# New figures in a kernel's list scheduler: traced durations, one DMA queue, hops between engines, GpSimd and two-operand VectorE work apart

## The chip, the cores and the metric

The kernel runs on one core of a Trainium2 chip. The metric is the device time of one execution in microseconds. The kernel before takes 753.49 us (median of 3 runs, 753.48 to 754.42).

## What is computed

Three layers follow each other, on 2 batches of 768 tokens, all in float32.

1. Clustered attention: 8 heads of 64. Each query and key is given to the nearest of 16 centroids (arg max of the cosine), and a query sees only the keys of its own cluster: `scores = where(q_assign == k_assign, q k^T / 8, -1e9)`, soft max, times v.
2. A mixture of 8 experts with one expert for a token: `e = argmax(x w_gate + modality_bias[modality_id])`, `out = gate * (relu(x w1[e]) w2[e])`, with w1 of 512 x 1024 and w2 of 1024 x 512.
3. A feed-forward layer of 2048: `h = x w_in`, `g = max(h, 0) + alpha * min(h, 0)`, `out = g w_out`. Its weights come as 64-bit floats and are turned into 32-bit ones on the chip.

## The kernel before

**Tiles and loops.** The attention goes by groups of two heads (4 groups in a batch), and in each by 12 units of 128 queries against 768 keys: the scores (`smm`, L946, in `pss`), the negated row maximum on VectorE (L953), the exponential on ScalarE (L965), a split of the result into two 16-bit parts (a high copy, then a low part on GpSimd, L393 on tile p, or on VectorE, L995), a DMA transpose of both parts issued by SyncE (L999, `pt<-p`), and the product with v on TensorE (`avm`, L1007 and L1009). A third of the first batch's units is transposed on TensorE instead. `group_prep` readies the next group meanwhile: transposes, norms (L756 is in that chain), nearest centroids (L840 to L847), the split of v (L913), and moves of 64 partitions to the other 64 (`move`), each on SyncE's DMA queue, GpSimd or ScalarE. After the last group of a batch `route` and `inverse` work out on VectorE, in a long chain of small operations, which token goes to which slot of which expert (the logits are added on L1070).

The experts work in slots of 128 tokens: SyncE loads the expert's weights in 8 parts (conditionally, where the expert is that of the slot before), GpSimd gathers the token rows (L1337), TensorE transposes them (L1345) and multiplies (L1401, L1431). The first 3 slots multiply in full float32; later ones (10) split the weights into a high part on ScalarE and a low part on VectorE (`whl`). GpSimd then gathers the rows back (L1447), TensorE transposes them (L1457), and the feed-forward runs by 16 slices of 128 of the inner 2048 for each batch: first product (L1517), leaky ReLU on VectorE (L1525, L1528), split (`ghl`, ScalarE and GpSimd), second product (L1545). Its weights are put together from 64-bit words on VectorE (L1487 to L1492) and split (`wf`).

**What sets the order.** Nothing of the order is written by hand. Each operation is declared with `S.op`: the engines that can do it with a cost each, what it reads and writes, a priority, and for a DMA its transfer time. `Sched.run` (L182) then plans the whole program on the host, and `emit` issues the operations in the order of their planned starts. Each engine executes its own queue strictly in that order, and waits with semaphores; so a wrong planned time costs nothing by itself, but an operation planned too early stands in the way of the ones behind it. In each step `run` works out for every ready operation the earliest start on its best engine (start + cost + a bias), takes for each engine, of those that start within a window of the earliest (0.03 us, on VectorE 0.3), the one with the lowest priority number, and plans of these the one that starts first. The plan is made in two parts: one up to a branch (L1657) at about 472 us, one for the last stage behind it.

The figures of the planner before: 0.2 us from an engine to any other (`LAT`), 0.127 between dependent VectorE operations, DMAs with an issue of 0.47 or 0.65, 0.65 more, their transfer (all transfers one after another, `dma_free`) and 0.9 to land. The dictionary `N` (L350) holds some fifty settings: ring sizes, offsets of priorities, biases.

Of the kernel before, what the change touches and what calls it, by code (L numbers as in the profile page):

```python
# [13 lines left out]
I32 = mybir.dt.int32  # L14
# [60 lines left out]
class Op:  # L75
    __slots__ = ("idx", "eng", "fn", "prio", "deps", "succ", "ndep", "ready", "start", "end", "bufs", "on", "dma", "bias", "adds", "slack")


class Sched:


    LAT = 0.2
    WIN = 3.41333
    SAME = 0.08
    DSAME = 0.127

    def __init__(self):
        self.ops = []
        self.prio = 0.0
        self.rings = []  # L90
        self.stream = None
        self.bias = {}
        self.win = {}
        self.back = 0.5
        self.warm = [False]
        self.pe_busy = {}
# [10 lines left out]
    def op(self, eng, fn, r=(), w=(), prio=None, dma=None, deps=(), bias=None, slack=0.0):  # L107
# [4 lines left out]
        o.prio = self.prio if prio is None else prio  # L112
# [6 lines left out]
        o.slack = slack  # L119
# [62 lines left out]
    def run(self, t0=0.0):  # L182
        ops = self.ops
        for o in ops:
            o.ndep = 0
            o.ready = t0
# [13 lines left out]
        dma_free = t0  # L200
        hw_free = t0
# [3 lines left out]
        while n_done < total:  # L205
            best = None
            per = {}
            for o in ready:
                at = o.ready
# [47 lines left out]
            end = self.pe_end(st, cost) if e == "PE" else st + cost  # L257
            free[e] = end
            if o.dma is not None and e in o.dma[2:] + (e,) * (len(o.dma) == 2):
                xfer, hw = o.dma[:2]  # L260
                if hw and e != "POOL":
                    hw_free = max(st, hw_free) + (0.47 if hw == "load" else 0.65)
                    xs = hw_free + 0.65
                    free[e] = hw_free + 0.03
                else:
                    xs = end + 0.65
                dma_free = max(xs, dma_free) + xfer
                if hw == "transpose":
                    free[e] = dma_free - 0.93
                end = dma_free + 0.9 + o.slack  # L270
            o.end = end
            ready.remove(o)
            n_done += 1
            for rg, i in o.adds:
                rg.free.append((end + self.LAT, i))
            for b in o.bufs:
                b.left -= 1
                if b.left == 0 and b.ring is not None:
                    b.ring.free.append((max(y.end for y in b.ops) + self.LAT, b.slot))
# [20 lines left out]
def kernel(  # L300
# [49 lines left out]
    N = dict(s1q=2, s1k=2, s2q=2, s2k=2, p=3, p16=5, pt=4, v16=2, wf_early=2, xs=2, whl=3, whl2=3, whi='A', wlo='D', lead=1, tw=1, wdma=1.25, pss=2, ps1=4, sq=1, bd=1.5, bp=0, ulead=4, pa=2, pb=0, nat=3, hi='*', lo='DP', lo0='PPT', vraw=1, mvp=1, mvb=0, epi=1, rM=2, lob=0.5, idle=40, pace=57, mve='PA', wd=0.3, wa=0.03, wp=0.03, wpl=0.03, cs=1, back=2, nld=8, dsame=0.127, lump='cs', mp=90, mps=8, mpn=0, trp=0.5, evp=3, xTs2=0, xtp=9, fl=6, rsh=1, rp0=0, go=-4, so=0, pre=0, fws=5, gs=4, gsl=1, xsl=0, eb=0.8)  # L350
# [4 lines left out]
    S.DSAME = N["dsame"]  # L355
# [22 lines left out]
    def chain(name, r, w, *steps, prio=None):  # L378

        if name in N["lump"]:  # L380
# [3 lines left out]
            S.op({"DVE": sum(0.127 + n / 960.0 for _, n in steps)}, all_, r=r, w=w, prio=prio)  # L384
            return
        for fn, n in steps:
            S.op({"DVE": 0.06 + n / 960.0}, fn, r=r, w=w, prio=prio)
# [10 lines left out]
    def open_pool(name, side="left", space=None, deps=()):  # L398
# [14 lines left out]
        o = S.op({"MEM": 0.0}, fn, deps=deps, prio=-1e9)  # L413
# [9 lines left out]
    def close_pool(name):  # L423
# [4 lines left out]
        return S.op({"MEM": 0.0}, lambda _: pools.pop(name).release(), deps=deps, prio=-1e9)  # L428
# [128 lines left out]
    def consts():  # L557
# [3 lines left out]
            name=nc.get_next_instruction_name(), act_func_set_id=6)), prio=-1e6)  # L561
        S.op({"POOL": 0.9}, lambda e: make_identity(nc, ident.t), w=[ident])
        S.op({"POOL": 0.1}, lambda e: nc.gpsimd.memset(half.t, 0.5), w=[half])
        S.op({"POOL": 0.1}, lambda e: nc.gpsimd.memset(cexp.t, CEXP), w=[cexp])
        S.op({"POOL": 0.1}, lambda e: nc.gpsimd.memset(tiny.t, 1e-30), w=[tiny])
        S.op({"POOL": 0.1}, lambda e: nc.gpsimd.memset(ones_r.t, 1.0), w=[ones_r])
        S.op({"DVE": 0.1}, lambda e: nc.vector.memset(one16.t, 1.0), w=[one16])

        S.op({"POOL": 0.2}, lambda e: iota(iw.t, [[-1, NCL]], NCL), w=[iw])
# [6 lines left out]
        S.op({"DVE": 0.3}, scales, w=[msc])  # L576
# [5 lines left out]
        for i in range(N["v16"]):  # L582
            S.op({"DVE": 0.1}, lambda e, i=i: nc.vector.memset(r_v16.tiles[i][:, :, :, 2 * D:], 1.0),
                 w=[(s2z, ("v", i))], deps=[r_v16.opened], prio=0)
# [3 lines left out]
    def zero(rg, i, view, n, key):  # L588
        S.op({"POOL": 0.1 + n / 1000.0, "DVE": c_dve(n)}, lambda e: ENG[e].memset(view(rg.tiles[i]), 0.0),
             w=[(s2z, key)], deps=[rg.opened])  # L590

    def late_consts():
        S.prio = 2
        S.op({"DVE": 0.2}, lambda e: nc.vector.memset(ones_b.t, 1.0), w=[ones_b])
        S.op({"POOL": 0.3}, lambda e: nc.gpsimd.affine_select(
            out=tri_b.t, in_=ones_b.t, pattern=[[1, P]], compare_op=ALU.is_gt, fill=0.0, base=0,
            channel_multiplier=-1), r=[ones_b], w=[tri_b])
        S.op({"POOL": 0.2}, lambda e: iota(iw8.t, [[-1, E]], E), w=[iw8])
        S.op({"POOL": 0.2}, lambda e: iota(tri8r.t, [[1, E], [-1, E]]), w=[tri8r])
# [1125 lines left out]
```

## Time and profile before

| | |
|---|---|
| median of the runs | 753.49 us |
| profiled execution | 755.47 us |
| its span, first to last instruction | 753.7 us |
| granted TensorE clock, mean | 0.97 |
| busy: TensorE, weight loads | 685.7, 578.5 us |
| busy: VectorE, ScalarE, GpSimd | 541.8, 397.2, 322.9 us |
| DMA | 101.39 MB, 135 GB/s |

The shares over the whole span hide that the stages have different limits; the table by stretches among the rows below has one line for each stage, with the busy time of every engine and the share of the DMA engines (1.0 is all 16 busy). Matmuls overlap, so a busy TensorE may still be below its best. A line such as L393 or L365 is that of a helper (a subtraction, a copy); there the names of the tiles tell the operations apart.

### The profile page before, as it was taken

The page shows a single profiled execution, that of the slowest core. Times are in us where ns is not written, and L with a number is a line of the kernel's source. Part 1 is how long each engine was busy: PE and PEld are TensorE (multiplying, and loading weights), DVE is VectorE, ACT ScalarE, POOL GpSimd, SP SyncE. Part 2 cuts the span into 40 slices and gives each one's busy share as a digit, 9 for nine tenths or more (in the row PEclk, how much of TensorE's full clock was granted, in tenths as well). Part 3 has the DMA queues.
Part 4 walks back from the last instruction along what each step waited for, and adds up shares of the span by engine and source line. Part 5 has one row for each costly group of instructions (what it writes and reads, how often), then busy time and mean ns, then how long its engine had stood idle before and what let it go on. Part 6 is the DMA issues. An engine that isn't in the chain of part 4 may idle for free. (4 is left out here: it accounts for less than half of the span.)

```text
span 753.7 us, 13656 instructions
## 1 busy us (share of the span) xinstructions
PE 685.7 (91%) x5041; PEld 578.5 (77%) x5041; DVE 541.8 (72%) x920; ACT 397.2 (53%) x609; POOL 322.9 (43%) x282
## 2 busy tenths in 40 slices
PE   8778889876888899989889999799999999999997
PEld 8768778765767657447668787699999889999996
DVE  7899889998978865399999896388988632322331
ACT  6778888854758667158769896122322231111112
POOL 5537776553648634001425400554556642222221
PEclk9999999996799999999999999899999999999999
DMA  7779998896999999940814913243343030000002
GB/s 182 174 145 208 168 170 184 150 229 107 220 217 230 189 173 195 294 160 29 292 57 140 330 61 128 77 132 115 115 142 135 14 108 19 1 0 1 1 1 85
DMA packets 167211, 101.39 MB, mean 135 GB/s; under 512 B 133120, under 2 KB 147840, under 8 KB 167136
## 3 DMA queue, kind: packets, MB, share of 16 engines
q1 hardware_dynamic: 164832, 93.04, 51.1%
q0 software_dynamic: 2304, 7.39, 3.6%
q8 instruction: 42, 0.69, 0.4%
q14 instruction: 33, 0.27, 0.1%
HBM read 87.37 MB, written 12.85 MB: 133 GB/s over the span
## 5 line engine op out<-in xcount | busy, mean ns | idle before, releaser
L1545 PE MATMUL ps<-wf,ghl 128*128 128x512 f32 x576 | 138.2, 392 | 1.6 <-POOL ghl L393 1.6
L1545 PEld LDWEIGHTS ps<-wf,ghl 128*128 128x128 f32 x576 | 107.1, 188 | 23.6 <-POOL ghl L393 3.0
L365 ACT ACTIVATE ghl<-g 128x384 fp32r<-128x384 f32 x64 | 33.7, 526 | 158.1 <-DVE g L1528 156.7
L393 POOL TENSOR_TENSOR ghl<-g,ghl 128x384 fp32r<-128x384 f32 x57 | 66.0, 1163 | 118.1 <-ACT ghl L365 118.1
L1525 DVE TENSOR_SCALAR m<-ps,alp 128x384 f32<-128x384 f32 x64 | 39.4, 615 | 106.4 <-PE ps L1517 106.4
L393 POOL TENSOR_TENSOR p<-p,p 128x768 f16<-128x768 f32 x57 | 97.0, 1711 | 37.1 <-ACT p L365 32.5
L965 ACT ACTIVATE p<-pss,nm 128x768 f32<-128x768 f32 x96 | 86.0, 898 | 34.3 <-DVE nm L953 16.3
L393 DVE TENSOR_TENSOR whl<-wst,whl 128x1024 fp32r<-128x1024 f32 x80 | 100.9, 1299 | 3.7 <-ACT whl L365 3.3
L953 DVE TENSOR_REDUCE nm<-pss 128x1 f32<-128x768 f32 x96 | 90.8, 950 | 15.8 <-PE pss L946 9.4
L365 ACT ACTIVATE whl<-wst 128x1024 fp32r<-128x1024 f32 x80 | 83.9, 1060 | 15.5 <-PE ps L1431 7.8
L1007 PEld LDWEIGHTS <-pt 128*128 128x128 f16 x1152 | 61.3, 100 | 34.5 <-DMA pt<-p 28.9
L1007 PE MATMUL ps<-v,pt 128*128 128x65 f16 x1152 | 69.9, 197 | 17.1 <-DMA pt<-p 16.1
L1517 PE MATMUL ps<-x2a,wf 128*128 128x384 f32 x384 | 72.1, 345 | 3.9 <-ACTq L1657 3.9
L946 PE MATMUL pss<-s1k,s1q 128*128 128x384 f32 x192 | 61.0, 400 | 14.4 <-ACT p L965 14.2
L1517 PEld LDWEIGHTS ps<-x2a,wf 128*128 128x128 f32 x384 | 69.9, 194 | 5.4 <-ACTq L1657 4.3
L1517 PE MATMUL ps<-x2b,wf 128*128 128x384 f32 x384 | 69.9, 338 | 0.0
L1517 PEld LDWEIGHTS ps<-x2b,wf 128*128 128x128 f32 x384 | 67.6, 188 | 1.1
L1401 PE MATMUL ps<-whl,xTs 128*128 128x512 f32 x240 | 64.0, 405 | 4.6 <-DVE whl L393 4.5
L1431 PE MATMUL ps<-whl,hTs 128*128 128x512 f32 x240 | 63.0, 399 | 3.1 <-DVE hTs L393 3.1
L1401 PEld LDWEIGHTS ps<-whl,xTs 128*128 128x128 f32 x240 | 45.1, 193 | 15.5 <-DVE whl L393 6.2
L393 POOL TENSOR_TENSOR wf<-tw,wf 128x1024 fp32r<-128x1024 f32 x16 | 40.1, 2507 | 35.5 <-ACT wf L365 35.3
L1431 PEld LDWEIGHTS ps<-whl,hTs 128*128 128x128 f32 x240 | 43.9, 188 | 14.7 <-DVE hTs L393 6.2
(244 smaller groups left out, 1214.4 us busy)
## 6 DMA issues: line engine op xcount, KB each, us to landing
wst<-in_moe_w_dram SPq DMA_DIRECT2D x104, 512.0 KB
wst<-in_moe_w_in_dram SPq DMA_DIRECT2D x8, 1024.0 KB
wst<-in_moe_w_out_dram SPq DMA_DIRECT2D x8, 1024.0 KB
ys_d<-ys SPq DMA_DIRECT2D x13, 256.0 KB
raw<-in_k_dram SPq DMA_DIRECT2D x8, 384.0 KB
raw<-in_q_dram SPq DMA_DIRECT2D x8, 384.0 KB
vraw<-in_v_dram SPq DMA_DIRECT2D x8, 384.0 KB
x_d<-xg SPq DMA_DIRECT2D x8, 384.0 KB
```

The lines of the kernel that those rows point to most:

```text
L365: nc.scalar.activation(out=out, in_=in_, func=AF.Copy)
L393: ENG[e].tensor_tensor(out=out, in0=a, in1=b, op=ALU.subtract)
L946: nc.tensor.matmul(s.t[:, jj, 0:HS], hd["12"[i], "q"].t[:, h, j, qs], hd["12"[i], "k"].t[:, h, jj], start=(i == 0), stop=(i == 1))
L953: S.op({"DVE": c_dve(SEQ)}, lambda e: nc.vector.tensor_reduce(out=nm.t, in_=s.t[:, :, 0:HS], axis=AX.XY, op=ALU.max, negate=True), r=[s], ...
L965: S.op({"ACT": c_act(SEQ) + 0.04}, lambda e: nc.scalar.activation(out=p.t, in_=s.t[:, :, 0:HS], func=AF.Exp, bias=nm.t), r=[s, nm], w=[p])
L1007: nc.tensor.matmul(o[:, c], pv, vv[:, D:VW], start=(i == 0), stop=(i == 2 * C - 1))
L1401: nc.tensor.matmul(hps[jj].t, lhs(xT, a, ci), rhs(ch, w_, cols), start=(ci == 0 and i == 0), stop=(ci == 3 and i == len(parts) - 1))
L1431: nc.tensor.matmul(yp.t, lhs(hT, a, f), rhs(4 + f // 2, w_, slice((f % 2) * 512, (f % 2 + 1) * 512)), start=(f == 0 and i == 0), stop=(f = ...
L1517: nc.tensor.matmul(hp.t[:, 0:HS], wi[:, a, kk, fs], x2b.t[:, bb, kk, sl], start=(n == 0), stop=(n == 3 * KD - 1))
L1525: S.op({"DVE": c_dve(HS) + 0.055}, lambda e: nc.vector.tensor_scalar(out=m.t, in0=hp.t[:, 0:HS], scalar1=0.0, scalar2=alp.t[:, f:f + 1], o ...
L1545: nc.tensor.matmul(view(), gh.t[:, a, tt * P:(tt + 1) * P], wo[:, bb, f % 2, :], start=(f == 0 and a == 0 and bb == 0), stop=(f == NF - 1 ...
```

## The change

The planner gets other figures; the operations, their buffers and priorities stay.

- Each engine has a time until others see its result (`SEEN`), and each pair of engines a hop (`HOP`). An operation's earliest start is kept for each engine that it may go to (`o.at`).
- There is one DMA queue: a transfer starts at its issue plus `ISSUE` (2.37 us for a transpose, 1.86 on SyncE, 1.9 on GpSimd) or when the one before has ended, takes its listed time and lands 0.13 later, with 0.05 until it is seen. SyncE is held for a listed time of its own, or until `LEAD` before the landing. A DMA's tuple gets a third number for that.
- Operations whose tag is in `TWO` (two operands from SBUF on VectorE) are not started before GpSimd is nearly done (0.1 us before), and GpSimd's computing operations not before such an operation ends.
- Listed durations change, among them: a transpose of the attention weights 1.345 to 1.91, a move 0.55 to 1.42, q, k and v loads 1.1 to 0.51, a first slot's weight load 2.95 to 3.44 for two parts, a conditional one 1.25 to 1.0 (`wdma`), a gather 0.75 to 0.9 (the extra 1.0 of `slack` is gone), scores 0.655 to 0.795, the product with v 0.51 to 0.55, a slot's matmuls 0.65 to 0.685 and 0.855 to 0.87, the last stage's 1.95 to 2.11 and 0.65 to 0.68, `wf` on GpSimd 1.01 to 1.92, `place` 0.6 to 0.99 on ScalarE.
- Every operation gets a name (`tag`) and `ORDER` and `TAIL` could add to its priority by name; both are empty.

```diff
 class Op:
-    __slots__ = ("idx", "eng", "fn", "prio", "deps", "succ", "ndep", "ready", "start", "end", "bufs", "on", "dma", "bias", "adds", "slack")
+    __slots__ = ("idx", "eng", "fn", "prio", "deps", "succ", "ndep", "ready", "start", "end", "bufs", "on", "dma", "bias", "adds", "tag", "two", "at")
+ORDER = {}
+TAIL = {}
+TWO = {"norm", "bias", "sims_eq", "sims_pos", "onehot", "v_lo", "p_lo", "w_lo", "wb2", "wb3", "wf_lo", "g_lo", "chain_h",
+       "chain_i", "chain_a", "chain_c", "chain_s", "chain_t", "chain_g"}
 class Sched:
-    LAT = 0.2
     WIN = 3.41333
-    SAME = 0.08
-    DSAME = 0.127
+    SEEN = {"PE": 0.165, "DVE": 0.085, "ACT": 0.105, "POOL": 0.035}
+    HOP = {("PE", "ACT"): 0.037, ("ACT", "POOL"): 0.1, ("PE", "DVE"): 0.106, ("DVE", "ACT"): 0.095, ("ACT", "DVE"): 0.033,
+           ("DVE", "PE"): 0.057, ("DVE", "POOL"): 0.08, ("POOL", "DVE"): 0.034, ("POOL", "PE"): 0.055, ("ACT", "PE"): 0.05,
+           ("PE", "POOL"): 0.1, ("POOL", "ACT"): 0.05, ("POOL", "SP"): 0.1}
+    FREED = 0.06
+    LANDED = 0.05
+    ISSUE = {"transpose": 2.37, "SP": 1.86, "POOL": 1.9}
+    LEAD = {"transpose": 2.91, "SP": 5.8}
...
-        o.prio = self.prio if prio is None else prio
+        o.prio = (self.prio if prio is None else prio) + self.order.get(tag, 0.0)
+        o.tag = tag
+        o.two = tag in TWO
...
                 for e, c in o.eng.items():
-                    st = max(at, free.get(e, t0))
+                    st = max(at, o.at[e], free.get(e, t0))
+                    if e == "DVE" and o.two:
+                        st = max(st, pool_till - 0.1)
+                    if e == "POOL" and not (o.dma and e in (o.dma[3:] or (e,))):
+                        st = max(st, dve_till)
                     cost = st + c + o.bias.get(e, 0.0)
...
-            end = self.pe_end(st, cost) if e == "PE" else st + cost
-            free[e] = end
-            if o.dma is not None and e in o.dma[2:] + (e,) * (len(o.dma) == 2):
-                xfer, hw = o.dma[:2]
-                if hw and e != "POOL":
-                    hw_free = max(st, hw_free) + (0.47 if hw == "load" else 0.65)
-                    xs = hw_free + 0.65
-                    free[e] = hw_free + 0.03
-                else:
-                    xs = end + 0.65
-                dma_free = max(xs, dma_free) + xfer
-                if hw == "transpose":
-                    free[e] = dma_free - 0.93
-                end = dma_free + 0.9 + o.slack
-            o.end = end
+            moved = o.dma is not None and e in (o.dma[3:] or (e,))
+            if moved:
+                xfer, kind, busy = o.dma[:3]
+                way = "transpose" if kind == "transpose" else e
+                dma_free = max(st + self.ISSUE[way], dma_free) + xfer
+                o.end = dma_free + 0.13
+                free[e] = st + 1.05 if e == "POOL" else max(st + busy, o.end - self.LEAD[way])
+            else:
+                free[e] = self.pe_end(st, cost) if e == "PE" else st + cost
+                o.end = free[e] + self.SEEN.get(e, 0.0)
+                if e == "DVE" and o.two:
+                    dve_till = free[e]
+                if e == "POOL":
+                    pool_till = free[e]
...
-                lat = {"DVE": self.DSAME, "PE": 0.0}.get(e, self.SAME) if e in s.eng and len(s.eng) == 1 and o.dma is None else self.LAT
-                s.ready = max(s.ready, end + lat)
+                for e2 in s.at:
+                    if moved:
+                        hop = self.LANDED
+                    elif e == e2:
+                        hop = -self.SEEN["PE"] if e == "PE" else 0.02
+                    else:
+                        hop = self.HOP.get((e, e2), 0.06)
+                    s.at[e2] = max(s.at[e2], o.end + hop)
...
-                 r=[(src, x) for x in K(sp_, sy)] + (zeros if z else []), w=[(dst, x) for x in K(part, y)], dma=(0.55, True, "SP"), bias=mv_bias)
+                 r=[(src, x) for x in K(sp_, sy)] + (zeros if z else []), w=[(dst, x) for x in K(part, y)], dma=(1.42, True, 0.6, "SP"), bias=mv_bias, tag="move")
...
-                 r=[(p16, 0), (p16, 1)], w=[pt], dma=(1.345, "transpose"))
+                 r=[(p16, 0), (p16, 1)], w=[pt], dma=(1.91, "transpose", 1.43), tag="turn")
...
-            r=[(inv, b), *xd[0:b + 1]], w=[xs], dma=(0.75, False), prio=p0 - 5, slack=N["xsl"])
+            r=[(inv, b), *xd[0:b + 1]], w=[xs], dma=(0.9, False, 0), prio=p0 - 5, tag="rows_in")
...
-            r=[(pos, b)] + ([ysd] if tiles is None else [(ysd, x) for x in tiles]), w=[yg], dma=(0.75, False), slack=N["gsl"])
+            r=[(pos, b)] + ([ysd] if tiles is None else [(ysd, x) for x in tiles]), w=[yg], dma=(0.9, False, 0), tag="rows")
```

## Rows read from the trace of the kernel before

**Rows 1.** Busy time by stretch: us, then busy and (count) of each engine, clock, DMA.

```profile
core 0: us, PE busy (x) PEld busy (x) DVE busy (x) ACT busy (x) POOL busy (x), PEclk, DMA share, GB/s
...
20.00:180.00 160.00, 131.94 (x1597) 114.85 (x1596) 147.43 (x317) 122.29 (x204) 97.90 (x90) 0.95 0.86 173
180.00:296.00 116.00, 100.77 (x1035) 78.90 (x1034) 90.75 (x162) 81.17 (x123) 65.53 (x55) 0.92 1.06 199
296.00:331.00 35.00, 32.63 (x218) 17.30 (x213) 16.59 (x90) 14.67 (x22) 4.37 (x3) 1.00 0.90 270
331.00:400.00 69.00, 61.32 (x281) 47.93 (x282) 68.06 (x65) 51.36 (x65) 19.41 (x11) 0.98 0.33 119
400.00:472.00 72.00, 68.93 (x340) 56.16 (x338) 59.53 (x62) 57.26 (x75) 15.90 (x14) 1.00 0.46 162
...
500.00:607.00 107.00, 106.58 (x546) 97.34 (x545) 88.33 (x98) 27.85 (x41) 57.52 (x35) 1.00 0.32 106
607.00:754.00 147.00, 142.09 (x715) 127.80 (x713) 40.01 (x68) 25.62 (x48) 36.99 (x38) 1.00 0.07 26
```

**Rows 2.** Line L999 on SyncE: duration ns min/median/max, first and last start us.

```profile
L999 SPq DMA_TRANSPOSE pt<-p x81: 1275/1757/4710, 31.4 to 302.5; - x81
```

**Rows 3.** Waits, whole span: us in total, times, longest us.

```profile
PEld L1007 <- DMA pt<-p: 28.9, 33, 2.5
...
PE ps L1007 <- DMA pt<-p: 16.1, 20, 2.3
```

**Rows 4.** Waits of VectorE, 20 to 310 us.

```profile
DVE nm L953 <- PE pss L946: 9.4, 18, 1.3
```

**Rows 5.** Groups of instructions, whole span: busy us, mean ns | idle before.

```profile
L393 DVE TENSOR_TENSOR whl<-wst,whl 128x1024 fp32r<-128x1024 f32 x80 | 100.9, 1299 | 3.7 <-ACT whl L365 3.3
...
L995 DVE SCALAR_TENSOR_TENSOR p<-p,p 128x768 f16<-128x768 f32 x24 | 27.2, 1140 | 1.7 <-POOL p L374 1.7
...
L913 DVE SCALAR_TENSOR_TENSOR v<-vraw,vsc,v 128x384 f16<-128x384 f32 x16 | 13.8, 905 | 0.8 <-ACT v L367 0.8
...
L756 DVE TENSOR_TENSOR rs<-rn,rs 128x24 f32<-128x24 f32 x8 | 7.2, 901 | 0.2
...
L847 DVE TENSOR_TENSOR sims<-iw,mx 128x384 f32<-128x384 f32 x8 | 5.8, 720 | 0.2
```

**Rows 6.** The same lines by themselves, and L1487: ns min/median/max.

```profile
L913 DVE SCALAR_TENSOR_TENSOR v<-vraw,vsc,v x16: 604/617/2005, 23.8 to 271.2; 128x384 f16<-128x384 f32 x16
...
L995 DVE SCALAR_TENSOR_TENSOR p<-p,p x24: 945/958/2282, 158.0 to 292.2; 128x768 f16<-128x768 f32 x24
...
L756 DVE TENSOR_TENSOR rs<-rn,rs x8: 182/590/3582, 13.0 to 250.1; 128x24 f32<-128x24 f32 x8
...
L1487 DVE TENSOR_SCALAR tw<-wst x16: 678/684/1500, 350.2 to 590.6; 128x1024 int32<-128x1024 int32 x16
...
L847 DVE TENSOR_TENSOR sims<-iw,mx x8: 557/559/1448, 18.6 to 255.1; 128x384 f32<-128x384 f32 x8
```

**Rows 7.** DMA issues, whole span: median us from issue to landing.

```profile
xs<-x_d,inv POOLq DMA_INDIRECT x13, 3.9
yg<-ys_d,posc POOLq DMA_INDIRECT x6, 3.9
yg<-ys_d,posu POOLq DMA_INDIRECT x6, 3.4
```

**Rows 8.** One of the moves: GpSimd's group of instructions, SyncE's DMA issues.

```profile
L374 POOL TENSOR_SCALAR s1k<-s1k 64x768 fp32r<-64x768 f32 x12 | 10.0, 830 | 15.7 <-ACT s1k L365 9.0 <-DMA s1k<-s1k 6.2
...
s1k<-s1k SPq DMA_DIRECT2D x6, 192.0 KB
```

**Rows 9.** VectorE in order of time at the attention's end: start, us, [idle before].

```profile
307.99 0.22 DVE L1017 TENSOR_SCALAR r<-ps,vsc 128x6 f32<-128x6 f32 x1 [10.78 <-PE ps L1007]
...
314.18 0.21 DVE L1070 TENSOR_TENSOR lgt<-ps,lgt 128x48 f32<-128x48 f32 x1 [5.15 <-PE ps L1066]
```

**Rows 10.** The chain that ended last, two of its repeating pieces: start, us.

```profile
733.34 4.10 PE ps L1545 x18
737.43 4.21 PE ps L1517 x24
```

More of the change, by code (lines that the diff above doesn't have):

```diff
@@ L94, in __init__ @@
         self.back = 0.5
+        self.order = ORDER
         self.warm = [False]
@@ L185, in run @@
             o.ndep = 0
-            o.ready = t0
+            o.at = {e: t0 for e in o.eng}
         cur = set(ops)
@@ L208, in run @@
             for o in ready:
-                at = o.ready
+                at = t0
                 ok = True
@@ L274, in run @@
             for rg, i in o.adds:
-                rg.free.append((end + self.LAT, i))
+                rg.free.append((o.end + self.FREED, i))
             for b in o.bufs:
@@ L278, in run @@
                 if b.left == 0 and b.ring is not None:
-                    b.ring.free.append((max(y.end for y in b.ops) + self.LAT, b.slot))
+                    b.ring.free.append((max(y.end for y in b.ops) + self.FREED, b.slot))
             for s in o.succ:
-                lat = {"DVE": self.DSAME, "PE": 0.0}.get(e, self.SAME) if e in s.eng and len(s.eng) == 1 and o.dma is None else self.LAT
-                s.ready = max(s.ready, end + lat)
+                for e2 in s.at:
[6 more added lines that the diff above has]
+                    s.at[e2] = max(s.at[e2], o.end + hop)
                 s.ndep -= 1
@@ L383, in all_ @@
                     fn(e)
-            S.op({"DVE": sum(0.127 + n / 960.0 for _, n in steps)}, all_, r=r, w=w, prio=prio)
+            S.op({"DVE": sum(0.155 + n / 960.0 for _, n in steps)}, all_, r=r, w=w, prio=prio, tag="chain_" + name)
             return
         for fn, n in steps:
-            S.op({"DVE": 0.06 + n / 960.0}, fn, r=r, w=w, prio=prio)
+            S.op({"DVE": 0.06 + n / 960.0}, fn, r=r, w=w, prio=prio, tag="chain_" + name)
     def dma(e, out, in_):
@@ L732, in low @@
                         op0=ALU.mult, op1=ALU.subtract)
-                S.op({"DVE": c_dve(HS)}, low, r=[tp] + [(t1, (y, 0, h)) for y in range(2)], w=[(tl, (y, z, h)) for y in range(2)])
+                S.op({"DVE": c_dve(HS)}, low, r=[tp] + [(t1, (y, 0, h)) for y in range(2)], w=[(tl, (y, z, h)) for y in range(2)], tag="low")
         rn = S.new(r_rn)
@@ L771, in place @@
                          src.rearrange("p (i x) n -> p i x n", i=1).to_broadcast([D, 2, 2, NCL]))
-        S.op({"ACT": 0.6, "DVE": 0.4, "POOL": 0.9}, place, r=[chl] + [(s2z, ("cs", i)) for i in range(N["cs"])], w=[cs])
+        S.op({"ACT": 0.99, "DVE": 1.99, "POOL": 1.14}, place, r=[chl] + [(s2z, ("cs", i)) for i in range(N["cs"])], w=[cs], tag="place")
         smt = S.new(r_smt)
@@ L786, in sm @@
                     n += 1
-        S.op({"PE": 12 * 0.163}, sm, r=[(pt["1", nm], k_) for nm in "qk" for y in range(2) for k_ in K(y, 0)]
-             + [(tl, k_) for tl, z in place_of.values() for y in range(2) for k_ in K(y, z)] + [cs], w=[sp])
-        S.op({"ACT": c_actp(HS), "DVE": c_dve(HS)}, lambda e: copy(e, smt.t, sp.t[:, 0:HS]), r=[sp], w=[smt])
+        S.op({"PE": 2.18}, sm, r=[(pt["1", nm], k_) for nm in "qk" for y in range(2) for k_ in K(y, 0)]
+             + [(tl, k_) for tl, z in place_of.values() for y in range(2) for k_ in K(y, z)] + [cs], w=[sp], tag="sm")
+        S.op({"ACT": c_actp(HS), "DVE": c_dve(HS)}, lambda e: copy(e, smt.t, sp.t[:, 0:HS]), r=[sp], w=[smt], tag="sims_out")
         zeros = [(s2z, (x, i)) for x in "qk" for i in range(N[f"s2{x}"])]
@@ L1009, in avm @@
                     nc.tensor.matmul(o[:, c, 0:D], pv, vv[:, 0:D], start=False, stop=False)
-        S.op({"PE": 0.51}, avm, r=[pt, (v16, (h, 0)), (v16, (h, 1))] + [(s2z, ("v", i)) for i in range(N["v16"])], w=[(a, c)])
+        S.op({"PE": 0.55}, avm, r=[pt, (v16, (h, 0)), (v16, (h, 1))] + [(s2z, ("v", i)) for i in range(N["v16"])], w=[(a, c)], tag="avm")
         if c < C - 1:
@@ L1032, in unit @@
         S.op({"DVE": c_dve(C * D), **({"ACT": 1.9} if N["epi"] else {})}, scaled,
-             r=[r] + [(a, i) for i in range(C)], w=[(xg, (y, h)) for y in range(2)], bias={"DVE": N["eb"]})
+             r=[r] + [(a, i) for i in range(C)], w=[(xg, (y, h)) for y in range(2)], bias={"DVE": N["eb"]}, tag="scaled")
     lps = {}
@@ L1519, in mm @@
                         n += 1
-            S.op({"PE": 1.95}, mm, r=[(x2b, (c, i)) for c in range(j * CH, (j + 1) * CH) for i in range(2)] + [(wb, 0), (wb, 1)], w=[hp])
+            S.op({"PE": 2.11}, mm, r=[(x2b, (c, i)) for c in range(j * CH, (j + 1) * CH) for i in range(2)] + [(wb, 0), (wb, 1)], w=[hp], tag="mm_first")
             m = S.new(r_m)
@@ L1645 @@
     t_end = S.end
+    S.order = TAIL
     def now():
```

243 lines of the change are left out of this document (120 added, 123 removed).

## The prediction

> **What bounds the kernel now.** I read the view by stretches first, then the waits of the two fullest engines, then the groups of instructions of single lines, then the chain that ended last. Read from the stretches [rows 1], the run has three regimes. From 20 to 180 us (attention, first batch) VectorE is the bound: 147.4 us busy of 160, with the DMA engines at 0.86. From 180 to 296 us (attention, second batch) no engine is full (VectorE 90.8 of 116), but the DMA share is 1.06: transfers bound it. From 296 to 331 us VectorE works 16.6 of 35, because the attention's end and the routing of the second batch are one chain. From 331 to 400 us VectorE is full again (68.1 of 69, the low halves of the expert weights), and from 400 to 472 us TensorE is (68.9 of 72). From 500 us on TensorE runs the last feed-forward almost without a hole (106.6 of 107, then 142.1 of 147). So 282 of the 754 us (472 to the end) can't become shorter by order alone, and a new order has the 311 us from 20 to 331 to win or lose in, with VectorE idle for 12.6, 25.3 and 18.4 us in its three stretches.
>
> The profiled execution took 755.47 us (span 753.7); the median of the runs is 753.49, which is 1.98 less. I sum against the first and subtract 1.98 at the end.
>
> **The change part by part.** No instruction's own work changes. The planner's figures do, and so the order on each engine and, where an operation may go to several engines, the engine. The tables of new priorities are empty, so every priority stays what it was. One choice in the planner matters for all that follows: it takes the operation with the earliest planned start, and priority decides only among starts within 0.03 us (0.3 on VectorE). Where an engine is full, everything ready starts at the same moment and the old priorities decide, as before; where it has holes, the planned times decide, and there the new figures count.
>
> *The DMA queue.* The old planner let a transpose of the attention weights land 0.65 + 0.65 + 1.345 + 0.9 = 3.55 us after its issue (3.75 with its hop), and a queue of them move at 1.345 each. The new one says 2.37 + 1.91 + 0.13 + 0.05 = 4.46, and 1.91 in a queue. SyncE is held a median of 1.757 us by each of the 81 transposes [rows 2], nearer to the new figure than to 1.345. That the old plan was too hopeful shows on TensorE, which runs in order: the product with the transposed weights (L1007) stood at the head of its queue and waited for that DMA 33 times, 28.9 us, in its weight loads and 20 times, 16.1 us, in its matmuls [rows 3]. With later planned landings these products go behind other work. TensorE isn't the bound there; what its waiting costs is what VectorE loses at the row maxima (L953), which waited for scores 18 times, 9.4 us [rows 4]. Bounds: 0 (the DMA engines bind anyway) and -9.4. I take half, -4.7, as the first-batch half of the attention is where VectorE is full and the second where the DMAs are.
>
> *GpSimd and two-operand VectorE work apart.* Such operations are stretched now: 16 of L913 with a mean of 905 ns against a shortest of 604, 24 of L995 with 1140 against 945, 8 of L756 with 901 against 182, 8 of L847 with 720 against 557 [rows 5, 6]. That is 4.8 + 4.7 + 5.8 + 1.3 = 16.6 us of VectorE, nearly all inside the attention. Planned apart, an operation is put off until GpSimd is done; that gains only if VectorE has another one ready, and only where VectorE is the bound. Bounds: 0 and -16.6. I take a quarter, -4.2. [...]
>
> [...]
>
> *Gathers.* The old figure for a row gather was 3.55 us from issue to use, with 1.0 more for those of the last stage. The new one is 1.9 + 0.9 + 0.13 + 0.05 = 2.98. The trace has medians of 3.9, 3.9 and 3.4 from issue to landing [rows 7], so the new plan is too short by 0.4 to 0.9 where the old was right or too long. Behind each stands a transpose on TensorE, and behind it in 400 to 472 us the bounding matmuls. The 13 gathers of the expert slots are issued two buffers ahead, which covers them; if that cover went, 13 x 0.9 = 11.7. The 12 of the last stage: at most 6 x 0.9 + 6 x 0.4 = 7.8. Bounds 0 and +19.5; I take +3, under half of the uncovered ones.
>
> *Moves between partition halves.* A DMA on SyncE now costs 1.42 in the queue instead of 0.55, so SyncE is planned as busy for longer and some moves go to GpSimd or ScalarE. GpSimd makes 12 of one kind at 830 ns, SyncE 6 [rows 8]. Each taken from SyncE frees a DMA engine share that is over-full and loads GpSimd, which feeds the transposes. Bounds: five moves one way or the other, -5 x 0.83 = -4 and +4; I take 0.
>
> *The end of the attention.* Between 297 and 314 us VectorE waits 10.8 us for the last product and 5.15 for the last logits [rows 9], while TensorE is full (32.6 of 35 [rows 1]) with the expert matmuls that the plan put between. The new figures move these in a way I can't work out by hand: bounds -8 (half of the two waits) and +10; taken as 0, and a rival below.
>
> *The last stage.* The planner's 2.11 and 0.68 us are what the chain shows: 4.21 for 24 matmuls of the first product, 4.10 for 18 of the second [rows 10]. With TensorE full, 0; bounds -2 and +4 (a stall at its start). The other durations (0.87 for a slot's matmuls, 1.92 for a GpSimd copy, 0.5 instead of 0.625 for a conditional weight load) move nothing that I can name.
>
> Sum: -4.7 - 4.2 + 3 + 0 + 0 + 0 = -5.9, so 755.47 - 5.9 = 749.6 in a profiled execution, and 749.6 - 1.98 = **747.6 us**.
>
> **Rivals.**
> *Slower: the end of the attention slips.* The new plan sees longer DMA delays, so it sees more holes on TensorE, and fills them with expert matmuls, which are ready early and which the old priorities hold back only among equal starts. On the chip these stand ahead of the last products, of the output transposes and of the logits, and the routing of the second batch starts later; behind it VectorE's 331 to 400 us are full, so what is late there is late at the end. For it: the 15.9 us of waits at that place are already of this kind [rows 9]. Against: part of the delay is the DMA's own. [...] It decides once the last logits are added after about 320 us (314.2 now).
> *Slower: the short gathers.* Cover of the slots' gathers goes: +11.7 instead of +3, which gives 755.47 - 8.9 + 11.7 - 1.98 = 756.3. For it: TensorE is full in 400 to 472 us. Against: the buffers two ahead.
> *No change.* What binds is the same work in the same priority order: VectorE's 12.6 idle us in 20 to 180, the DMA engines above 1.0 behind it. Both gains are 0 and the gathers are covered: 753.5. [...]
> *A larger gain.* All of the 9.4, half of the 16.6, gathers covered: -17.7 with nothing lost at the end of the attention, 735.8; half way from the forecast, about 741, is what I give it.
>
> **How the numbers follow.** Chances: forecast 0.36 (its own range 743 to 751.5), larger gain 0.14, no change 0.12, slipped end 0.23, short gathers 0.15. A measurement of this kernel can tell 0.2%, 1.5 us. Faster by more than that: 0.36 + 0.14 = 0.50; within: 0.12; slower: 0.38. The range goes from 738 (past the middle of the larger gain) to 765 (past the slipped end) and leaves out some 0.13.
>
> **What would show it.** Right: L1007's waits for DMA well below 28.9 and 16.1; L953's below 9.4; the means of L913, L995 and L756 near their shortest; the stretch after 472 us still 280 us. Wrong: waits of the gathers' transposes on TensorE in 400 to 472 us; the last logits after 320 us; new VectorE idle time in 20 to 180 us, which would mean that planning apart left holes that nothing filled.

## The result, and the profile after

The changed kernel takes 767.1 us (median of 4 runs, 762.19 to 768.69) against 753.49 before: 1.0148 of its time, 95% interval 1.012 to 1.0176. It is slower, and the forecast of 747.6 was wrong in sign. The profiled execution is the quickest of the four, 762.19 us with a span of 760.5, so between the two profiles the loss is 6.7 us, half of the 13.6 us between the medians. Of the other half, 4.9 us lie between this execution and the median of the changed kernel, and 2.0 us come from the profile before, which is an execution above its own median. A longer execution of the changed kernel was profiled in the first experiment. An execution more than 1.5% above the quickest of its kernel is left out of the times below; this concerns one, of 789.8 us.

The stretches of the changed kernel, in the columns and the cuts of [rows 1]:

```profile
20.00:180.00 160.00, 136.46 (x1632) 118.76 (x1629) 137.98 (x318) 132.54 (x216) 94.31 (x88) 0.96 0.86 171
180.00:296.00 116.00, 91.37 (x1025) 74.94 (x1025) 92.43 (x167) 85.47 (x126) 57.68 (x44) 0.91 1.02 194
296.00:331.00 35.00, 30.51 (x157) 16.88 (x158) 18.57 (x92) 6.11 (x11) 1.04 (x1) 0.85 0.80 258
331.00:400.00 69.00, 68.63 (x302) 50.32 (x302) 57.29 (x55) 56.82 (x74) 12.10 (x7) 1.00 0.36 124
400.00:472.00 72.00, 69.45 (x346) 56.53 (x345) 62.34 (x65) 60.67 (x83) 15.87 (x12) 1.00 0.49 172
...
607.00:754.00 147.00, 144.78 (x733) 130.59 (x732) 43.10 (x73) 25.62 (x47) 36.63 (x37) 1.00 0.05 16
```

Read TensorE (first pair) first. From 180 to 296 us it does 91.4 us of work where it did 100.8, from 296 to 331 us 30.5 where it did 32.6: 11.5 us of work are missing there, and from 331 to 400 us it is full (68.6 of 69) where it had 7.7 us to spare. VectorE, which was full there (68.1), now has 57.3. Work of TensorE was put off from a place where it had room to one where it has none.

It is the work with the unsplit weights of the first three expert slots. The same stretches with TensorE's instructions on these weights alone, before:

```profile
180.00:296.00 116.00, 24.24 (x46) 7.92 (x46) 0.00 (x0) 0.00 (x0) 0.92 1.06 199
331.00:400.00 69.00, 0.00 (x0) 0.00 (x0) 60.07 (x48) 37.80 (x36) 0.98 0.33 119
```

and after:

```profile
180.00:296.00 116.00, 11.28 (x20) 3.72 (x20) 0.00 (x0) 0.00 (x0) 0.91 1.02 194
331.00:400.00 69.00, 12.33 (x28) 4.79 (x27) 49.98 (x42) 41.08 (x40) 1.00 0.36 124
```

13.0 us less of it are done up to 296 us, and 12.3 us of it stand behind 331 us, where none stood. The times of single instructions tell the same (us from the start of the span; row maxima, logits and last matmul at their end, the others at their start):

| | before | after |
|---|---|---|
| 48th row maximum (half of the attention) | 145.6 | 147.5 |
| last row maximum of the attention | 297.0 | 287.3 |
| last logits added | 314.4 | 309.7 |
| first expert slot stored | 298.7 | 314.0 |
| third expert slot stored | 329.0 | 346.4 |
| first matmul of a slot with split weights | 330.5 | 344.0 |
| last matmul of such a slot | 470.8 | 475.4 |
| first matmul of the last stage | 474.7 | 479.4 |
| end | 753.7 | 760.5 |

The attention did end sooner, by 9.7 us at its last row maximum and 4.7 at the logits. The three unsplit expert slots, which share TensorE with it, ended 15 to 17 us later. SyncE's queue shows why. Its instructions in order of time (start, us, what, how many in a row), before:

```profile
245.37 0.73 SPq L1331 DMA_DIRECT2D wst<-in_moe_w_dram  x1
246.15 0.62 SPq L1047 DMA_DIRECT2D x_d<-xg  x1
249.32 0.11 SPq L1331 DMA_DIRECT2D wst<-in_moe_w_dram  x1
249.55 12.46 SPq L999 DMA_TRANSPOSE pt<-p  x5
...
264.91 1.78 SPq L1331 DMA_DIRECT2D wst<-in_moe_w_dram  x5
267.00 15.63 SPq L999 DMA_TRANSPOSE pt<-p  x7
```

and after:

```profile
247.04 0.49 SPq L1353 DMA_DIRECT2D wst<-in_moe_w_dram  x1
248.57 6.45 SPq L1021 DMA_TRANSPOSE pt<-p  x3
255.07 2.38 SPq L412 DMA_DIRECT2D s2q<-mt  x2
257.57 21.57 SPq L1021 DMA_TRANSPOSE pt<-p  x10
279.19 0.58 SPq L1069 DMA_DIRECT2D x_d<-xg  x1
279.88 18.32 SPq L1021 DMA_TRANSPOSE pt<-p  x9
298.42 2.29 SPq L1353 DMA_DIRECT2D wst<-in_moe_w_dram  x3
```

Before, the eighth weight load of the first slot was issued at 245.4 us, and six of the second slot by 266.7. After, the fifth of the first slot goes out at 247.0 and the sixth at 298.4, behind the 22 transposes that end the attention. From 247 to 298 us TensorE makes 4 matmuls with unsplit expert weights, where it made 34 before.

The planner's rule for it stands in an unchanged line: a load may not start before `dma_free - back`, with the old setting `back=2`. Behind a transpose's issue the old queue stood 0.65 + 0.65 + 1.345 = 2.6 us ahead, so a load was held for 0.6 us; the new one stands 2.37 + 1.91 = 4.3 us ahead, so it is held for 2.3. What decides is when SyncE itself is free again in the plan. Before, that was 1.7 us after the issue (2.6 less 0.93), when the hold was over, so a load and the next transpose could be planned for the same moment and the priority chose. Now it is 1.5 us (4.3 and 0.13 less `LEAD`, 2.91), and the hold lasts 0.8 us longer: where the next transpose, which is not held, is ready by then, it is planned first each time. This is worked out from the two planners' lines; the experiments with `back` test it.

TensorE's granted clock differs there as well. The same columns in steps of 5 us, before:

```profile
296.00:301.00 5.00, 4.94 (x65) 3.17 (x61) 1.17 (x3) 3.93 (x6) 2.90 (x2) 1.00 1.11 232
301.00:306.00 5.00, 4.74 (x45) 2.49 (x44) 0.00 (x0) 0.11 (x1) 1.47 (x2) 1.00 1.09 185
```

after:

```profile
286.00:291.00 5.00, 2.35 (x56) 2.13 (x54) 2.22 (x4) 3.38 (x4) 1.97 (x1) 0.90 1.20 166
291.00:296.00 5.00, 3.13 (x58) 2.57 (x55) 0.97 (x3) 0.84 (x1) 3.24 (x2) 0.76 1.07 210
296.00:301.00 5.00, 2.85 (x46) 2.53 (x47) 0.00 (x0) 0.00 (x0) 0.00 (x0) 0.58 1.05 202
301.00:306.00 5.00, 2.66 (x15) 1.35 (x13) 0.97 (x3) 0.00 (x0) 0.00 (x0) 0.50 0.99 349
306.00:311.00 5.00, 5.00 (x25) 3.50 (x24) 1.24 (x6) 0.98 (x2) 0.00 (x0) 0.89 0.27 82
```

After the change TensorE is busy for 2.35 to 3.13 us of each step from 286 to 306 us and the granted clock goes down from 0.90 to 0.50; from 306 us on the engine is full, with 0.89 in the first step and 1.00 from 311 to 321 us. Before, with 4.94 and 4.74 us busy, it is 1.00.

### The profile page after: what moved, and what is told of

It reads as the page before. It is cut to its first block, busy times and chain, and to the rows that moved or that the text cites. A ratio compares the mean times of both kernels' runs of the same rounds, so it can differ in the third digit from the quotient of the medians.

```text
span 760.5 us, 13689 instructions
## 1 busy us (share of the span) xinstructions
PE 690.7 (91%) x5041; PEld 583.9 (77%) x5041; DVE 521.7 (69%) x912; ACT 416.0 (55%) x631; POOL 301.8 (40%) x267
## 5 line engine op out<-in xcount | busy, mean ns | idle before, releaser
L415 POOL TENSOR_TENSOR p<-p,p 128x768 f16<-128x768 f32 x57 | 95.0, 1674 | 54.2 <-ACT p L387 51.7
L415 POOL TENSOR_TENSOR ghl<-g,ghl 128x384 fp32r<-128x384 f32 x63 | 70.6, 1130 | 106.0 <-ACT ghl L387 106.0
L415 DVE TENSOR_TENSOR whl<-wst,whl 128x1024 fp32r<-128x1024 f32 x80 | 95.8, 1225 | 10.9 <-ACT whl L387 10.7
L1029 PE MATMUL ps<-v,pt 128*128 128x65 f16 x1152 | 70.6, 198 | 13.3 <-DMA pt<-p 12.3
L415 POOL TENSOR_TENSOR wf<-tw,wf 128x1024 fp32r<-128x1024 f32 x16 | 38.4, 2399 | 53.8 <-ACT wf L387 53.8
L968 PEld LDWEIGHTS pss<-s1k,s1q 128*128 128x128 f32 x192 | 31.5, 203 | 32.3 <-ACT p L987 31.6
L1359 POOL DMA_INDIRECT xs<-x_d,inv x13 | 17.5, 1345 | 93.0 <-PE ps L1367 72.0
```

Source lines behind the costliest of these rows:

```text
L415: ENG[e].tensor_tensor(out=out, in0=a, in1=b, op=ALU.subtract)
L968: nc.tensor.matmul(s.t[:, jj, 0:HS], hd["12"[i], "q"].t[:, h, j, qs], hd["12"[i], "k"].t[:, h, jj], start=(i == 0), stop=(i == 1))
L1029: nc.tensor.matmul(o[:, c], pv, vv[:, D:VW], start=(i == 0), stop=(i == 2 * C - 1))
L1359: S.op({"POOL": 1.05}, lambda e: nc.gpsimd.indirect_dma_start(out=xs.t, out_offset=None, in_=x_d[0:(b + 1) * SEQ, :], in_offset=bass.Indir ...
```

## The experiments

Each was timed beside the kernel before on the same chip, which took 756.4 us beside the changed kernel again, `back=6`, `back=0.5` and the kernel without the rules, 755.7 beside the held loads, both mends together and the two with `w_load`, and 757.6 beside the gathers' line alone and the rules alone. My theory: late weight loads cost the time. Rivals: the rules that hold GpSimd and VectorE apart, the short gathers, or all of the new figures together.

**The changed kernel again.**

> The changed kernel once more, to see how far its executions spread and whether a slower one shows where its extra microseconds lie. All theories: 762 to 769 us. If the spread is TensorE's clock, an execution that takes 4 us or more longer shows a lower granted clock in a stretch between 180 and 350 us, and the same order of work.

Measured 765.2 us, 1.011 (1.0055 to 1.0164), between 762.6 and 771.1. Its profile is one of the long executions (span 769.4, 8.9 more than the first), and shows a part of what made it long:

```profile
306.00:311.00 5.00, 2.14 (x13) 1.14 (x11) 0.97 (x3) 0.00 (x0) 0.00 (x0) 0.50 0.97 336
311.00:316.00 5.00, 5.00 (x18) 3.66 (x17) 0.00 (x0) 0.98 (x2) 0.00 (x0) 0.50 0.10 23
316.00:321.00 5.00, 5.00 (x21) 2.75 (x22) 1.40 (x7) 0.00 (x0) 0.00 (x0) 0.50 0.98 357
321.00:326.00 5.00, 5.00 (x11) 2.17 (x11) 4.36 (x27) 0.60 (x1) 0.00 (x0) 0.88 0.28 110
```

Here the clock stays at 0.50 for ten microseconds in which TensorE is full, and is 0.88 in the next five. Counted by the clock that is 2.5 + 2.5 + 0.6 = 5.6 us of its work, an estimate, against 0.55 in the first profile (0.89 from 306 to 311 us). 5.0 us had been lost by the last row maximum (292.3 against 287.3), 4.3 of them by the 48th (151.8 against 147.5), and the first split matmul is 10 us later (354.0). Where those first 5 us went is not shown.

**Loads let go earlier** (the changed kernel, `back` as far as the new queue reaches).

```diff
-back=2
+back=6
```

> The changed planner, with the expert weights' loads allowed up to 6 us behind the planned end of the DMA queue instead of 2; nothing else. Theory of the starved loads: slot 0's eight loads stand before the 59th transpose again (in the changed kernel three of them stand behind the 81st), its result is stored before 300 us (314 now), the first matmul of a split slot starts at 330 us or earlier (344 now), and the time falls by 8 to 18 us, to 748 to 758. Rival, GpSimd and VectorE kept apart leave holes: the order there stays, so the time stays at 760 to 768.

Measured 764.3 us, 1.0108 (1.0065 to 1.015). The slot is stored at 279.0 us (before 298.7) and the first split matmul starts at 331.0 (330.5), so the mechanism is undone, and yet nearly nothing is won: a miss. Two things take its place. From 331 to 400 us VectorE is full again (68.5 of 69 us), as before the change; and ScalarE, which makes the high weights and the inputs of the next product, stands still from 415 us on (start, us, what, idle time before it and what ended it):

```profile
413.01 2.01 ACT L387 ACTIVATE whl<-wst 128x1024 fp32r<-128x1024 f32 x2 [0.90 <-PE ps L1453]
420.07 0.72 ACT L389 ACTIVATE yg<-yg,gate 128x512 f32<-128x512 f32 x1 [5.04 <-DMA yg<-ys_d,posc]
420.69 0.58 ACT L1432 ACTIVATE hb<-ps 128x512 f32<-128x512 f32 x1
```

A gathered row tile is scaled on ScalarE; the gather was issued at 413.41 us and is planned to land 3 us later, and the engine waits for it until 420.07, with the ReLU behind it ready. TensorE then waits 4.27 us for that ReLU.

**Loads held in the kernel before** (its figures are all old; the last part of slot 0 and all of slot 1 wait for the last attention unit).

```diff
-                 deps=[] if pace is None else [units[pace + c0]])
+                 deps=[units[pace + c0 if c0 < 5 else 95]] if pace is not None else [units[95]] if (b, j) == (0, 1) else [])
```

> The planner and the figures of before. Only the DMA queue's order is changed: the last three weight loads of expert slot 0 and all of slot 1 may not be planned before the scores of the last attention unit, so that they stand behind the 76th transpose or later, about as in the changed kernel. Theory of the starved loads: slot 0 is stored at 310 us or later (298.7 before), the first split slot starts at 342 us or later (330.5), and the time rises by 5 to 12 us. Rival, it is the rest of the new order (attention, routing, gathers) that costs: the time rises by 3 us at most.

Measured 766.7 us, 1.015 (1.0115 to 1.0185): as much as the whole change loses, by this alone. Its stretches are those of the changed kernel:

```profile
180.00:296.00 116.00, 93.42 (x1016) 76.47 (x1015) 95.01 (x165) 84.25 (x125) 63.87 (x52) 0.90 1.02 196
296.00:331.00 35.00, 31.91 (x189) 17.02 (x189) 16.57 (x90) 5.29 (x10) 1.37 (x2) 0.88 0.86 258
331.00:400.00 69.00, 66.83 (x294) 48.97 (x293) 61.14 (x57) 54.36 (x69) 14.94 (x9) 1.00 0.40 139
```

First slot stored at 312.4 us (after: 314.0), first split matmul at 344.4 (344.0), end at 760.3 (760.5).

**The gathers' landing mended, alone and with the loads.**

```diff
-                o.end = dma_free + 0.13
+                o.end = dma_free + 0.13 + (0.9 if o.tag in ("rows", "rows_in") else 0.0)
```

With `back=6`:

> The changed planner with the loads' limit 6 as in back6, and each row gather planned to land 0.9 us later (3.88 us instead of 2.98, the traced median is 3.9); nothing else. Theory of the short gathers: the waits of ScalarE and GpSimd for gathered rows fall from 23 us in back6 (12.0 + 11.0) to below 10, the 25 us between two slots that ScalarE's wait at 415 us made in back6 goes, and the time falls by 5 to 9 us, to 755 to 760. Rival, VectorE binds from 331 to 400 us whatever the gathers do: no more than 2 us below back6.

Measured 757.9 us, 1.0024 (1.0001 to 1.0047); 6.4 less than with the loads alone, and the two intervals do not overlap. The waits for the rows that are gathered back fell less than I expected, from 23.0 to 18.5 us, but they changed the engine: on ScalarE from 11.9 to 4.4 us, on GpSimd from 11.1 to 14.1. The stores of the slots around 415 us lay 18.3 and 19.3 us apart with `back=6` alone and lie 14.8 and 16.6 apart here, and the last split matmul is at 467.8 us, against 475.7.

The same line with `back=2`, as in the changed kernel:

> The changed kernel with only its planned gathers landing 0.9 us later (3.88 us from issue to use in place of 2.98); the loads of the expert weights stay as late as in the changed kernel (five of the first slot's ahead of transpose 59, none more until transpose 81). Before takes about 755.7 and the changed kernel about 765 beside it. Theory A, the two losses are partly one: behind late slots TensorE is full from 331 us on (68.6 of 69, 69.5 of 72 us), so no gather's wait is left to take away there; the mend brings 0 to 3 us, 762 to 765. Rival B, the losses add: as between the two kernels with the loads let go earlier the mend brings 6 us, so 757 to 760. Either way the first expert slot is stored after 310 us and the first slot with split weights starts after 342 us; if they come earlier the comparison says nothing on gathers.

Measured 767.0 us, 1.0123 (1.0089 to 1.0158): nothing won, as theory A had it. Its first slot is stored at 319.1 us, and TensorE is then full:

```profile
331.00:400.00 69.00, 69.00 (x300) 49.17 (x297) 57.97 (x65) 54.29 (x70) 12.08 (x7) 1.00 0.43 147
```

So either mend by itself is worth about 0 (1.0108 and 1.0123, where the change has 1.011 and 1.0148) and both together 7 to 9 us: where one bound is lifted the other holds.

**Only the weight loads let go early**, with and without the gathers' line (loads of q, k and v keep `back=2`).

```diff
-                    at = max(at, dma_free - self.back)
+                    at = max(at, dma_free - (6.0 if o.tag == "w_load" else self.back))
```

> The changed planner; only the expert weights' loads get the limit of 6 us, those of q, k and v keep 2. The order of the DMA queue has all loads of slot 0 and 1 before the 69th transpose, earlier than any kernel so far. Starved loads: slot 1 is stored before 312 us and the first split slot starts at 330 us or earlier; the time is 750 to 758 if nothing is lost behind it, 758 to 765 if the short gathers cost as in back6. Rival, loads in the middle of the transposes delay the attention: the last row maximum ends after 300 us (287 to 292 in the changed kernel) and the gain is used up.

> Both mends at once: the expert weights' loads with a limit of 6 us, q, k and v with 2, and gathers planned to land 0.9 us later. If both theories hold, this is the fastest of the four, at or below the kernel before on the same chip: 748 to 756 us. If only the loads mattered, it equals the kernel with the loads' limit alone.

Measured 779.1 us, 1.0296 (1.026 to 1.0332), and 772.2, 1.0217 (1.0188 to 1.0246): both forecasts of a gain missed, and the rival held. Now the weight loads go out ahead of the loads that the attention needs: the last two loads of v are issued at 262.0 and 304.6 us, where the changed kernel has 206.3 and 243.0. The first slot is stored at 264.5 us, and the last row maximum is at 327.2 (after: 287.3). VectorE's row maxima wait for scores in the first of the two kernels (us, times, longest), where [rows 4] had 9.4 us:

```profile
DVE nm L975 <- PE pss L968: 37.8, 26, 10.5
```

The gathers' line is worth 6.9 us here; the two profiles show 5.3 of them between the first and the last split matmul (157.6 against 162.9 us).

**A shorter hold in the kernel before.**

```diff
-back=2
+back=0.5
```

> The planner of before, all its old figures, with the loads allowed only 0.5 us behind the planned end of the DMA queue instead of 2: four of slot 0's loads stand behind the 59th transpose and three behind the 81st, as in the changed kernel. Starved loads: slot 0's result is stored after 310 us (298.7 before), the first split slot starts near 344 us, the time rises by 8 to 14 us, to 761 to 768. Rival, the new figures themselves or the keeping apart: none of them is in this kernel, so 753 to 756.

Measured 793.6 us, 1.0509 (1.0451 to 1.0567). The sign is as expected and the size three times as large. Here the loads of q, k and v are held too: the last two of v go out at 229.4 and 264.3 us, not 197.9 and 233.9, the last row maximum is at 304.0 us and the first slot is stored at 329.3. How the 37 us divide between these loads and those of the expert weights is not shown. The hold against the planned queue is a strong setting in the old planner as well.

**GpSimd and VectorE no longer apart** (the changed kernel without these lines).

```diff
-                    if e == "DVE" and o.two:
-                        st = max(st, pool_till - 0.1)
-                    if e == "POOL" and not (o.dma and e in (o.dma[3:] or (e,))):
-                        st = max(st, dve_till)
```

> The changed planner without the two rules that keep GpSimd and two-operand VectorE work apart; everything else new, the loads' limit 2. The order of the DMA queue shifts with it: slot 0's last load stands before the 69th transpose. Rival, keeping apart leaves holes: the time returns to 750 to 756 and VectorE's busy time between 20 and 180 us falls. Starved loads: slot 0 is stored near 305 us, in the middle, and the time is 755 to 763; the stretched operations (L935, L1017 and the norms, 604, 945 and 182 ns at their shortest) go back to means like those of before, 905, 1140 and 901.

Measured 787.5 us, 1.0423 (1.0372 to 1.0475), above both forecasts. The stretching comes back in part: the means of L931, L1013 and L774 are 935, 1025 and 753 ns, with the rules 763, 1004 and 325. Taking the rules away does not give the loss back, but what they win or cost can't be read from it: the plan's load order changes as well (the first slot's first two loads go out 41 and 61 transposes in, its last one 69, not 81), and the attention ends 29.4 us later. That they do not cause the loss shows better in the kernel with `back=6` and the gathers' line, which has them and takes 1.0024.

**These rules alone in the kernel before** (its figures old, the same four lines and the list of operations added).

> The kernel before with one part of the change alone: its planner keeps all its old figures, and only holds two-operand VectorE work and GpSimd work apart. Loads of the expert weights are not starved by it (eight ahead of transpose 53, twelve ahead of 59; before: eight ahead of 59, fourteen ahead of 65). Before takes about 755.7 beside it. Theory A (my term of -4.2 in the forecast): the stretched operations get shorter, the second operand's waits are filled with other work, 749 to 754. [...] Rival C: with the old figures of time the two are planned apart where the chip doesn't have them apart, holes stay empty and the attention ends later than 297 us: 758 to 770.

Measured 765.4 us, 1.011 (1.008 to 1.0139): rival C, and the attention ends later than 297 us (last row maximum at 301.8). Most of the stretching is gone (ns, shortest, median, longest; compare [rows 6]):

```profile
L1009 DVE SCALAR_TENSOR_TENSOR p<-p,p x24: 941/951/2289, 164.1 to 302.9; 128x768 f16<-128x768 f32 x24
...
L770 DVE TENSOR_TENSOR rs<-rn,rs x8: 174/183/957, 13.8 to 252.8; 128x24 f32<-128x24 f32 x8
...
L861 DVE TENSOR_TENSOR sims<-iw,mx x8: 549/559/560, 19.5 to 262.6; 128x384 f32<-128x384 f32 x8
```

and the time comes back as waiting:

```profile
20.00:180.00 160.00, 131.43 (x1545) 114.26 (x1546) 134.97 (x308) 126.67 (x214) 95.31 (x84) 0.96 0.79 165
```

VectorE is busy 12.5 us less than in [rows 1] in these 160 us and does fewer instructions (308, not 317); its 48th row maximum ends at 149.8 us, not 145.6, and it waits 24.9 us for scores instead of 9.4.

## Why the prediction was wrong

**The step that failed is "The end of the attention", taken as 0.** No term of the sum counts the loads of the expert weights. I bounded this one by the waits of VectorE, and its rival had the opposite mechanism: TensorE would be filled with too many expert matmuls, and the logits would come late. They came 4.7 us early (309.7, under the 320 from which that rival decides), because TensorE had too few. What I missed is one rule, to be worked through with the new figures: the hold of a load is counted from the planned end of the DMA queue, 2 us before it. Behind a transpose the old plan has SyncE free 0.93 us before that end, when the hold is over, the new one 2.78 us before it, when it is not. I wrote that the new load durations "move nothing that I can name" and looked at the durations of the loads, not at the queue they wait for. The kernel before with late loads loses the same 1.5%. The gains of the sum did not come either: with both mends the changed planner still takes 1.0024 of the time before, so nothing of -4.7 and -4.2 is left over there.

How the delay comes through: 13.5 us at the first split matmul (344.0 against 330.5), 4.6 at the end of these slots, since TensorE with its work piled up runs a slot in 12.9 us (eight stored between 373.2 and 476.1) where one took 13.4 before, at first with VectorE full (363.9 and 471.5); then +2.0 in the last stage. That is 6.8 us of span. The rest, up to the 13.6 of the medians, is in how the executions spread: the profile before is 2.0 us above its median, the profile after 4.9 below. In one longer execution an estimated 5.0 us more than in the first profile (5.6 less 0.55) went where TensorE was full at a clock below 1.00; what the others lost was not seen.

**What bounds the kernel.** I took VectorE from 331 to 400 us as the bound behind the routing, and everything late before it as late at the end. The stretch has two nearly full engines, within 8 us of each other: VectorE 68.1 and TensorE 61.3 with the three slots done early, TensorE 68.6 and VectorE 57.3 with them late. TensorE's 100.8 and 32.6 us [rows 1] before 331 us were not filler to be moved at no cost, they were what kept the next stretch free.

**The DMA queue, -4.7.** Products that stand and wait for their transpose did become rarer; in the changed kernel (us, times, longest, as in [rows 3, 4]):

```profile
PEld L1029 <- DMA pt<-p: 17.0, 19, 2.8
...
DVE nm L975 <- PE pss L968: 15.0, 20, 2.4
...
PE ps L1029 <- DMA pt<-p: 12.3, 12, 2.6
```

against 28.9 and 16.1. But the row maxima wait 15.0 us for scores, not less than 9.4: the gain did not go where the term said. One reading in the term was wrong too: a queue of transposes did not move at 1.345 each in the old plan but at 1.715 (0.65 + 0.65 + 1.345 less the 0.93 by which SyncE is let go early), and the measured hold of 1.757 [rows 2] is nearer to that than to 1.91. The old plan's queue was near the trace. That its landing was short is an estimate from the waits, 28.9 and 16.1 us with 3.55 planned, 17.0 and 12.3 with 4.46; when a transpose lands no view shows. With the expert slots in place (`back=6` and the gathers' line) the last row maximum is at 292.5 us and the logits at 311.9, 4.5 and 2.5 us sooner than before. By the second batch's table of slots it is lost again (333.3 against 330.9): the way there takes 21.4 us, not 16.5, and in it now stand three low halves of expert weights, which stood behind the routing before (busy us and mean ns, then idle us before them, from 311.6 to 333.4 us of that kernel).

```profile
L415 DVE TENSOR_TENSOR whl<-wst,whl 128x1024 fp32r<-128x1024 f32 x3 | 3.7, 1220 | 0.2 <-issue 0.2
```

**GpSimd and VectorE apart, -4.2.** The first half of the term is right: in the changed kernel L935 and L1017, the L913 and L995 of [rows 6], are seldom stretched. Of the 16.6 us some 7.5 are left: the means are 763, 1004, 325 (L778, before L756) and 836 ns (L869, before L847), and only the last one rose.

```profile
L935 DVE SCALAR_TENSOR_TENSOR v<-vraw,vsc,v x16: 605/616/1612, 25.0 to 262.8; 128x384 f16<-128x384 f32 x16
...
L1017 DVE SCALAR_TENSOR_TENSOR p<-p,p x24: 945/950/2164, 159.4 to 287.6; 128x768 f16<-128x768 f32 x24
...
L1509 DVE TENSOR_SCALAR tw<-wst x16: 684/1401/1485, 325.9 to 593.6; 128x1024 int32<-128x1024 int32 x16
```

The second half is wrong: VectorE's busy time from 20 to 180 us fell by 9.4 us and its idle time rose by as much, to 22.0, which the prediction had named as the sign against it; half of the attention is done at 147.5 us, not 145.6. The upper of the term's two bounds, 0, was nearer than my -4.2; in the old planner the rules alone measured above 0, at +1.1%. The last line is an operation with one input, which the change's list leaves out: its median went from 684 ns [rows 6] to 1401. From 500 to 607 us it lies beside a full TensorE (107.0 of 107 us busy), and I put no time down to it.

**Gathers, +3.** The mechanism is right, planned too short, and a wrong engine was named: I had a transpose on TensorE behind each gather, but half of the scalings (6 of 12) moved to ScalarE, where the ReLU and the weights stand behind them. The size is 6 to 7 us with the loads let go early and about 0 in the changed kernel, whose slots are late. Six of the twelve gathers that I gave to the last stage are issued before it, from 397.9 to 426.1 us, and the old 3.55 us for the slots' gathers was short as well, by 0.35. In the last stage a late gather stands on the chain that ended last (start, us, what):

```profile
480.83 4.49 DMA yg<-ys_d,posu
...
485.41 0.78 POOL yg L396
486.19 1.94 POOL ghl L415
...
488.17 4.18 PE ps L1567 x16
```

GpSimd waits for the rows, and the low part of the first activations (`ghl`), which TensorE needs, stands behind it. TensorE stands for 1.5 us there; at the same place it stood for 1.2 before. I had put the last stage at 0 with bounds of -2 and +4; it takes 281.1 us from its first matmul, where it took 279.1. That the gathers cost these 2.0 us is not shown: with their line it takes 279.5 with `back=2` and 281.3 with `back=6`, and 280.0 in the second profile of the changed kernel.

**Moves** stay at 0: no run tells them apart from the rest.

**The rivals.** Two of their figures are slightly off: half way from 747.6 to 735.8 is 741.7, not about 741, and the 765 that was to lie past the slipped end does so only without the +3 of the gathers (+10 us with both gains at nothing: 755.47 + 10 - 1.98 = 763.5, with it 766.5).

## What to carry to other kernels

A planner's settings are fitted to its figures: where a figure becomes more exact, look for every rule that is counted from it (here a hold of 2 us before the planned end of a queue) and work out what the old number now means. In a stretch that looks bound by one engine, ask what the others get done there that the next stretch would have to do, and look at the queue that feeds them. And a mend that measures 0 by itself is not shown to be worthless while a second bound stands beside it.

## What the runs showed of the hardware

Two things I had not expected. TensorE's clock was low while the engine was full: in the second profile of the changed kernel it was full from 311 to 321 us at 0.50, while in the first, with the same instructions in the same order, the clock was at 0.89 over the first five microseconds of full work (306 to 311 us). In the first profile two matmuls with unsplit weights (128x512) took 1.22 and 1.06 us at 0.50 (304.0 and 305.0 us) and ten at 1.00 (from 313.1 us) 0.59 each, 0.43 apart. In the first comparison four executions of the changed kernel lay 6.5 us apart and four of the kernel before 1.5; when it was timed again, 8.5 (four) and 9.3 (eleven). And a gather can take nearly twice its median: of the 13 with a median of 3.9 us from issue to landing in [rows 7] the longest took 7.5, and where ScalarE waited above it was 6.7 us from the issue, 2.2 us behind another gather and among seven weight loads, until ScalarE began.
